# Persistent zero-padded buffers, smaller first LayerNorm batches and memsets on GpSimd in a linear-attention plus MLP kernel

## The chip, the cores and the metric

One core of a Trainium2 chip runs the whole kernel. The engines are TensorE (PE, with its weight loads shown apart as PEld), VectorE (DVE), ScalarE (ACT), GpSimd (POOL) and SyncE (SP), which issues the DMAs. The metric is the time of one execution in microseconds (us) on the device; of several executions the median is taken.

## The reference

The input x has 2048 rows of 640 bfloat16 values. Each row is normalised (mean and variance over 640, eps 1e-5), and the result xn goes into two branches that are added to x:

```
q, k, v  = xn @ wqkv                    # 32 heads of 20
pq, pk   = phi(q), phi(k)               # phi(t) = (t > 0 ? t + 1 : exp(t)) + 1e-6
kv, z    = sum over rows of pk v^T, of pk      # per head
A        = ((pq kv) / (pq z + 1e-6)) @ wo
B        = max(xn @ w1, 0) @ w2         # 640 -> 1728 -> 640
out      = x + A + B
```

## The kernel before, in words

Rows are worked on in 16 tiles of 128 rows; four tiles make a group of 512 rows. The 640 attention columns are cut into six groups of heads, five of 120 columns and one of 40, and the 1728 hidden columns of the MLP into 13 chunks of 128 and one of 64.

**Loads.** SP issues x tiles 0 to 3 one by one (L87), then wqkv (L89), then x in three pieces of four tiles (L91), then w1, w2 and wo. Rows of w2 and wo beyond the last real one are zeroed on POOL.

**Stage 1 and 2 (tiles).** `ln_stats(tg)` computes the statistics of four tiles on DVE: two `bn_stats` (L162) and one `bn_aggr` (L163) per tile, then for the four tiles together the inverse square root, as eps plus variance (`vpe`, L165), a shift and a multiply-add on the bits (`yi`, `y0i`), and three Newton steps of four operations each (L177 to L188). These are 15 short operations on 128x4 values, each needing the one before. `phase_a(t)` normalises a tile on DVE (`xn`, L198), transposes it with five PE matmuls against `ident` into PSUM (`tp`, L204) and copies it on ACT into `xnT` (L205). `phase_b(t)` computes k and v of the tile (ten matmuls each, L212 and L220), phi(k) with an exp on ACT (L227), a min on DVE (L229) and a max-add on DVE (`pk_all`, L230), and copies v into `v_aug` on ACT (L235, L241), which has one extra column of ones per head group so that the next stage also yields z. k_ps and v_ps share three PSUM buffers. So v_ps of tile t+1 takes the buffer of k_ps of tile t, free when `pk_all` of tile t is done, and k_ps of tile t+2 takes that of v_ps of tile t. In the text k_ps(4) is the k_ps of tile 4, and so on.

The loop goes over t with a lag of two tiles between phase a and phase b; `ln_stats` of group 1 stands in front of phase_a(1), of group 2 in front of phase_a(5), of group 3 in front of phase_a(9).

**Stage C.** For each head group, 16 matmuls accumulate kv over all tiles (L312). The result is masked into `KVmask` and `Zh`, which had been zeroed by DVE memsets (L270, L273). `hind`, `et` and `Amat` are 0/1 patterns made on POOL.

**Stage 3 (groups of 512 rows).** q and phi(q) (L341 to L358), the MLP's hidden chunks (`do_h`, L363 to L378), the denominator and its reciprocal (L384 to L398), the numerator (L403 to L416), and per tile the sum over 14 hidden chunks and six head groups into `o_ps` (L418 to L439), plus x, and the store. The operands of these matmuls are read at all 128 partitions, so wherever a tile has fewer real rows, `zero_pad` (L76) clears the rest. That happens on DVE each time for `pq` (L354), the last hidden chunk (L374), `rden` (L397) and `o` (L412).

**Order.** The planner (the tile framework) decides each engine's order when the kernel is built. Among the instructions whose inputs are ready in its own reckoning it takes the one that stands earliest in the program. So short work that stands late, such as the memsets of L270, is drawn forward into idle time, and steps of a dependent chain have other instructions between them.

Of the kernel before, what the change touches and what calls it, by code (L numbers as in the profile page):

```python
# [7 lines left out]
ALU = mybir.AluOpType  # L8
# [4 lines left out]
def kernel(  # L13
# [10 lines left out]
    nc = tc.nc  # L24
    bf16 = mybir.dt.bfloat16
# [4 lines left out]
    S, D = x2.shape  # L30
# [102 lines left out]

    xnT = xpool.tile([P, NC, S], bf16, name="xnT")

    kvin_ctx = ExitStack()
    kvin = kvin_ctx.enter_context(tc.tile_pool(name="kvin", bufs=1))
    ctxAB = ExitStack()
# [3 lines left out]
    pk_all = kvin.tile([P, NT, D], bf16, name="pk_all")  # L142
    v_aug = kvin.tile([P, NT, NG, GW + 1], bf16, name="v_aug")
    if D // GW > 0:
        nc.vector.memset(v_aug[:, :, 0 : D // GW, GW : GW + 1], 1.0)
    if NG > D // GW:
        gs, w = groups[-1]
        nc.vector.memset(v_aug[:, :, NG - 1, w : w + 1], 1.0)

    i32 = mybir.dt.int32  # L150
    lnp = ctxAB.enter_context(tc.tile_pool(name="lnp", bufs=2))
    mv_alls = {}
    rstds = {}

    def ln_stats(tg):
        mv_all = lnp.tile([P, TPG, nc.vector.BN_AGGR_DIM], f32, name="mv_all")
        for ti in range(TPG):
            t = tg * TPG + ti
            stats = wk1.tile([P, 2, nc.vector.BN_STATS_DIM], f32, name="stats")
            xr = x_all[:, t, :].rearrange("p (n f) -> p n f", n=2)  # L160
            for i in range(2):
                nc.vector.bn_stats(stats[:, i, :], xr[:, i, :])  # L162
            nc.vector.bn_aggr(mv_all[:, ti, :], stats[:])  # L163
        vpe = wk1.tile([P, TPG], f32, name="vpe")
        nc.vector.tensor_scalar(vpe[:], mv_all[:, :, 1], 1e-5, None, op0=ALU.add)  # L165
        yi = wk1.tile([P, TPG], i32, name="yi")
        nc.vector.tensor_single_scalar(
            yi[:], vpe[:].bitcast(i32), 1, op=ALU.arith_shift_right
        )
        y0i = wk1.tile([P, TPG], i32, name="y0i")  # L170
        nc.vector.tensor_scalar(
            y0i[:], yi[:], -1, 0x5F3759DF, op0=ALU.mult, op1=ALU.add
        )
        y = y0i[:].bitcast(f32)
        for it in range(3):
            t1 = wk1.tile([P, TPG], f32, name="nt1")
            nc.vector.tensor_tensor(t1[:], y, y, ALU.mult)  # L177
            t2 = wk1.tile([P, TPG], f32, name="nt2")
            nc.vector.tensor_tensor(t2[:], t1[:], vpe[:], ALU.mult)
            t3 = wk1.tile([P, TPG], f32, name="nt3")  # L180
            nc.vector.tensor_scalar(
                t3[:], t2[:], -0.5, 1.5, op0=ALU.mult, op1=ALU.add
            )
            if it < 2:
# [3 lines left out]
            nc.vector.tensor_tensor(yn[:], y, t3[:], ALU.mult)  # L188
            y = yn[:]
        mv_alls[tg] = mv_all  # L190
        rstds[tg] = yn

    def phase_a(t):
        tg, ti = divmod(t, TPG)
        mv_all = mv_alls[tg]
        rstd = rstds[tg]
        xn = wk1.tile([P, D], bf16, name="xn")
        nc.vector.tensor_scalar(  # L198
            xn[:], x_all[:, t, :], mv_all[:, ti, 0:1], rstd[:, ti : ti + 1],
            op0=ALU.subtract, op1=ALU.mult,  # L200
        )
        tp = ps_tp.tile([P, NC, P], bf16, name="tp")
        for c in range(NC):
            nc.tensor.transpose(tp[:, c, :], xn[:, c * P : (c + 1) * P], ident[:])  # L204
        nc.scalar.copy(xnT[:, :, t * P : (t + 1) * P], tp[:])  # L205
# [36 lines left out]

    LAG = 2
    ln_stats(0)
    for t in range(NT + LAG):
        if t < NT:
            if t % TPG == 1 and t // TPG + 1 < NTG:
                ln_stats(t // TPG + 1)
            phase_a(t)
        if t >= LAG:  # L250
            phase_b(t - LAG)
# [15 lines left out]
    for g, (gs, w) in enumerate(groups):  # L267
        h0 = gs // Dh
        kvm = const.tile([P, P], bf16, tag=f"kvm{g}", name=f"kvm{g}")
        nc.vector.memset(kvm[:], 0.0)  # L270
        KVmask.append(kvm)
        zh = const.tile([P, H], bf16, tag=f"zh{g}", name=f"zh{g}")
        nc.vector.memset(zh[:], 0.0)  # L273
        Zh.append(zh)
        hind = const.tile([P, H], bf16, tag=f"hind{g}", name=f"hind{g}")
        nc.gpsimd.memset(hind[:w, :], 1.0)
        nc.gpsimd.affine_select(  # L277
            out=hind[:w, :], in_=hind[:w, :], pattern=[[-Dh, H]],
            compare_op=ALU.is_ge, fill=0.0, base=Dh * h0, channel_multiplier=1,
        )  # L280
# [7 lines left out]
        nc.gpsimd.memset(et[:], 0.0)  # L288
# [36 lines left out]
    kvin_ctx.close()  # L325

    with ExitStack() as ctx3:
        qo = ctx3.enter_context(tc.tile_pool(name="qo", bufs=2))
        hp = ctx3.enter_context(tc.tile_pool(name="hp", bufs=2))
        wk2 = ctx3.enter_context(tc.tile_pool(name="wk2", bufs=3))  # L330
        opool = ctx3.enter_context(tc.tile_pool(name="opool", bufs=3))
# [3 lines left out]
        for tg in range(NTG):  # L335
            tsl = slice(tg * TG, (tg + 1) * TG)
            pq = []
            for g, (gs, w) in enumerate(groups):
                q_ps = psA.tile([P, 512], f32, tag="mm", name="q_ps")
                for c in range(NC):  # L340
                    nc.tensor.matmul(  # L341
                        q_ps[:w, :TG],
                        wqkv_sb[:, c, gs : gs + w],
                        xnT[:, c, tsl],
                        start=(c == 0), stop=(c == NC - 1),
                    )
                eq = wk2.tile([P, TG], bf16, name="eq")
                nc.scalar.activation(eq[:w, :], q_ps[:w, :TG], ACT.Exp)  # L348
                eq1 = wk2.tile([P, TG], bf16, name="eq1")
                nc.vector.tensor_scalar(  # L350
                    eq1[:w, :], eq[:w, :], 1.0, 1e-6, op0=ALU.min, op1=ALU.add
                )
                pqt = qo.tile([P, TG], bf16, tag=f"pq{g}", name=f"pq{g}")
                zero_pad(nc.vector, lambda lo, hi: pqt[lo:hi, :], w)  # L354
                nc.vector.scalar_tensor_tensor(
                    pqt[:w, :], in0=q_ps[:w, :TG], scalar=0.0, in1=eq1[:w, :],
                    op0=ALU.max, op1=ALU.add,
                )  # L358
                pq.append(pqt)
# [44 lines left out]
            for g, (gs, w) in enumerate(groups):  # L404
# [68 lines left out]
```

## Time and profile before

| what | value |
|---|---|
| median of 6 executions | 269.38 us (269.06 to 270.0) |
| the profiled execution | 269.81 us, span 268.1 us |
| PE busy | 248.6 us, 93% of the span |
| DVE busy | 133.2 us, 50% |
| ACT busy | 104.5 us, 39% |
| POOL busy | 13.1 us, 5% |
| first transpose on PE | 11.93 us |
| first k matmul | 13.91 us |
| end of the kv matmuls of stage C | about 71.5 us |

The profile is one execution, seen by the hardware profiler. The span runs from its first to its last instruction; the execution's time is a little longer than that. Times in timelines are counted from the span's start. In a row of forty digits each digit is the busy share of one fortieth of the span, 6.7 us, in tenths. A row of waits names the waiting engine and line, what released it, the total, the number of waits and the longest. The chain is followed back from the last instruction, at each step to what released it. In the table by stage each line is a stretch of time, its length, and the busy time and instruction count of PE, PEld, DVE, ACT and POOL, then the granted clock and the DMA share and rate.

### The profile page before, as it was taken

What the parts mean: (1) busy time and instruction counts of PE and PEld (TensorE: products, weight loads), DVE (VectorE), ACT (ScalarE), POOL (GpSimd) and SP (SyncE); (2) the same over time, 40 slices, a digit from 0 to 9 for tenths busy, and PEclk for the clock granted to TensorE, in tenths of its full rate; (3) what the DMA queues carried; (4) which work ended last, traced back from release to release, by engine and by line L of the source; (5) the groups of instructions that cost most, each with busy time, mean ns of one, the idle gap of its engine ahead of it and who ended that gap; (6) DMA issues with size and microseconds to landing.
All of it is one profiled execution on the core that took longest, in us unless ns stands there. A gap on an engine that the chain in (4) does not pass through costs nothing.

```text
span 268.1 us, 3982 instructions
## 1 busy us (share of the span) xinstructions
PE 248.6 (93%) x1609; PEld 132.6 (49%) x1609; DVE 133.2 (50%) x350; ACT 104.5 (39%) x179; POOL 13.1 (5%) x59
## 2 busy tenths in 40 slices
PE   0187899999999999999999999999999999999994
PEld 0154555656844445565444555544455564445552
DVE  6869996335795766128254511844341154235211
ACT  1153676665356660005666100465710035563000
POOL 8900000000000000000000000000000000000000
PEclk9999999999999999999999999999999999999999
DMA  6999900000000000000000000000001000000010
GB/s 202 390 388 375 187 5 2 0 4 0 4 0 0 2 0 24 27 24 24 0 2 0 26 27 24 24 2 0 0 0 51 24 24 4 0 0 0 27 49 24
DMA packets 8219, 13.19 MB, mean 49 GB/s; under 512 B 457, under 2 KB 6921, under 8 KB 8201
## 3 DMA queue, kind: packets, MB, share of 16 engines
q1 hardware_dynamic: 8201, 12.95, 14.5%
q8 instruction: 12, 0.20, 0.3%
q14 instruction: 6, 0.05, 0.1%
HBM read 10.32 MB, written 2.62 MB: 48 GB/s over the span
## 4 chain that ended last, share of the span: by engine, by line
PE 83%; DVE 10%; DMA 5%; SPq 1%; issue 0%; ACT 0%; DVEq 0%
PE h_ps L367 23%; PE o_ps L425 23%; PE q_ps L341 10%; PE o_ps L433 10%; DMA x_all<-in_A_x_dram 5%; PE v_ps L220 5%; PE k_ps L212 4%; DVE stats L162 3%; PE num_ps L410 2%; PE rep_ps L406 2%; DVE pk_all L230 2%; PE den_ps L386 2%; PE kv_ps L312 2%; DVE xn L198 1%; PE tp L204 1%; SPq L87 1%
## 5 line engine op out<-in xcount | busy, mean ns | idle before, releaser
L367 PE MATMUL h_ps<-xnT,w_sb 128*128 128x512 bf16 (+1 forms) x280 | 62.3, 380 | 0.0
L367 PEld LDWEIGHTS <-w_sb 128*128 128x128 bf16 (+1 forms) x280 | 26.7, 99 | 35.1 <-issue 5.1
L348 ACT ACTIVATE eq<-q_ps 120x512 bf16<-120x512 f32 (+1 forms) x24 | 14.3, 596 | 74.9 <-PE q_ps L341 74.9
L441 DVE TENSOR_TENSOR o_sb<-o_ps,x_all 128x640 bf16<-128x640 f32 x16 | 13.2, 825 | 53.4 <-PE o_ps L433 53.3
L341 PE MATMUL q_ps<-xnT,wqkv_sb 128*120 128x512 bf16 (+1 forms) x120 | 27.0, 379 | 0.3 <-ACT kvsb L318 0.3
L220 PE MATMUL v_ps<-wqkv_sb,xnT 128*128 128x512 bf16 (+1 forms) x160 | 24.5, 299 | 2.6 <-DVE pk_all L230 2.6
L395 DVE RECIPROCAL rdenf<-denp 32x512 f32<-32x512 f32 x4 | 13.4, 3341 | 25.6 <-ACT denp L391 25.6
L212 PE MATMUL k_ps<-wqkv_sb,xnT 128*128 128x512 bf16 (+1 forms) x160 | 25.3, 306 | 0.0
L341 PEld LDWEIGHTS <-wqkv_sb 128*120 128x120 bf16 (+1 forms) x120 | 14.7, 127 | 10.8 <-issue 1.8
L204 PE MATMUL tp<-ident,xn 128*128 128x128 bf16 x80 | 7.7, 236 | 12.9 <-POOL hind_977 L277 11.9
L220 PEld LDWEIGHTS <-xnT 128*128 128x128 bf16 x160 | 13.0, 98 | 12.1 <-issue 2.9
L212 PEld LDWEIGHTS <-xnT 128*128 128x128 bf16 x160 | 13.3, 100 | 10.1 <-issue 1.3
L162 DVE BATCH_NORM_STATS2 stats<-x_all 128x6 f32<-128x320 bf16 x32 | 14.1, 468 | 3.7 <-DMA x_all<-in_A_x_dram 3.7
L205 ACT COPY xnT<-tp 128x640 bf16<-128x640 bf16 x16 | 11.1, 707 | 11.7 <-PE tp L204 11.7
L235 ACT CAST v_aug<-v_ps 128x600 bf16<-128x600 f32 x16 | 10.5, 658 | 12.9 <-PE v_ps L220 12.9
L408 ACT CAST rep<-rep_ps 120x512 bf16<-120x512 f32 (+1 forms) x24 | 13.5, 580 | 2.3 <-PE rep_ps L406 1.6
L227 ACT ACTIVATE ek<-k_ps 128x640 bf16<-128x640 f32 x16 | 11.2, 703 | 7.1 <-PE k_ps L212 7.1
L204 PEld LDWEIGHTS <-xn 128*128 128x128 bf16 x80 | 5.6, 106 | 13.7 <-DVE xn L198 13.2
L198 DVE TENSOR_SCALAR xn<-x_all,mv_all,rstd 128x640 bf16<-128x640 bf16 x16 | 7.0, 454 | 0.3 <-PE tp L204 0.2
L312 PE MATMUL kv_ps<-v_aug,pk_all 128*120 128x121 bf16 (+1 forms) x96 | 5.1, 213 | 0.0
L312 PEld LDWEIGHTS <-pk_all 128*120 128x120 bf16 (+1 forms) x96 | 5.0, 128 | 0.1
L78 POOL MEMSET wo_sb<- 32x640 bf16 (+1 forms) x7 | 4.1, 626 | 0.2
(586 smaller groups left out, 444.9 us busy)
## 6 DMA issues: line engine op xcount, KB each, us to landing
out_dram<-o_sb SPq DMA_DIRECT2D x16, 160.0 KB, 1.8
wqkv_sb<-in_A_wqkv_dram SPq DMA_DIRECT2D x1, 2400.0 KB
w_sb<-in_B_w_dram SPq DMA_DIRECT2D x1, 2160.0 KB, 14.7
w_sb<-in_B_w_dram SPq DMA_DIRECT2D x1, 2080.0 KB, 22.3
x_all<-in_A_x_dram SPq DMA_DIRECT2D x3, 640.0 KB, 13.6
wo_sb<-in_A_wo_dram SPq DMA_DIRECT2D x1, 750.0 KB, 11.9
x_all<-in_A_x_dram SPq DMA_DIRECT2D x4, 160.0 KB, 2.6
w_sb<-in_B_w_dram SPq DMA_DIRECT2D x1, 80.0 KB, 18.4
```

What stands on the lines that cost most here:

```text
L162: nc.vector.bn_stats(stats[:, i, :], xr[:, i, :])
L204: nc.tensor.transpose(tp[:, c, :], xn[:, c * P : (c + 1) * P], ident[:])
L212: nc.tensor.matmul(k_ps[:, cs : cs + n], xnT[:, c, t * P : (t + 1) * P], wqkv_sb[:, c, D + cs : D + cs + n], start=(c == 0), stop=(c == NC ...
L220: nc.tensor.matmul(v_ps[:, cs : cs + n], xnT[:, c, t * P : (t + 1) * P], wqkv_sb[:, c, 2 * D + cs : 2 * D + cs + n], start=(c == 0), stop= ...
L312: nc.tensor.matmul(kv_ps[:w, 0 : w + 1], pk_all[:, t, gs : gs + w], v_aug[:, t, g, 0 : w + 1], start=(t == 0), stop=(t == NT - 1),)
L341: nc.tensor.matmul(q_ps[:w, :TG], wqkv_sb[:, c, gs : gs + w], xnT[:, c, tsl], start=(c == 0), stop=(c == NC - 1),)
L348: nc.scalar.activation(eq[:w, :], q_ps[:w, :TG], ACT.Exp)
L367: nc.tensor.matmul(h_ps[:m, :TG], w1_sb[:, c, fs : fs + m], xnT[:, c, tsl], start=(c == 0), stop=(c == NC - 1),)
L395: nc.vector.reciprocal(rdenf[:H, :], denp[:H, :])
L408: nc.scalar.copy(rep[:w, :], rep_ps[:w, :TG])
L425: nc.tensor.matmul(o_ps[:, cs : cs + n], hT[j][:, ti * P : (ti + 1) * P], w2_sb[:, j, cs : cs + n], start=(step == 0), stop=(step == nstep ...
L433: nc.tensor.matmul(o_ps[:, cs : cs + n], oT[g][:, ti * P : (ti + 1) * P], wo_sb[:, g, cs : cs + n], start=(step == 0), stop=(step == nstep ...
```

## The change

A new pool `pers` holds two sets of `pq`, `o`, `rden` and last hidden-chunk buffers for the whole kernel. Their padding rows are zeroed once, on POOL, right after `xnT` is allocated, and stage 3 takes set `tg % 2`. The 68 `zero_pad` calls' memsets of stage 3 fall away, and 34 on POOL take their place. The memsets of `v_aug`'s ones, of `kvm` and of `zh` go from DVE to POOL. The statistics are computed in five batches, of tiles 0-1, 2-3, 4-7, 8-11 and 12-15, with two Newton steps instead of three. A batch stands in front of the phase a of the tile before its first: batch 1 in front of phase_a(1), batch 2 in front of phase_a(3), batch 3 in front of phase_a(7), batch 4 in front of phase_a(11).

```diff
+    pers = ctx.enter_context(tc.tile_pool(name="pers", bufs=1))
+    pq_bufs, o_bufs, rden_bufs, hlast_bufs = [], [], [], []
+    for b in range(2):
+        pqb, ob = [], []
+        for g, (gs, w) in enumerate(groups):
+            tpq = pers.tile([P, TG], bf16, tag=f"pq{g}_{b}", name=f"pq{g}_{b}")
+            zero_pad(nc.gpsimd, lambda lo, hi, tpq=tpq: tpq[lo:hi, :], w)
+            pqb.append(tpq)
+            tob = pers.tile([P, TG], bf16, tag=f"ot{g}_{b}", name=f"ot{g}_{b}")
+            zero_pad(nc.gpsimd, lambda lo, hi, tob=tob: tob[lo:hi, :], w)
+            ob.append(tob)
...
+        trd = pers.tile([P, TG], bf16, tag=f"rden_{b}", name=f"rden_{b}")
+        zero_pad(nc.gpsimd, lambda lo, hi, trd=trd: trd[lo:hi, :], H)
...
+            zero_pad(nc.gpsimd, lambda lo, hi, thl=thl: thl[lo:hi, :], ml)
...
-        nc.vector.memset(v_aug[:, :, 0 : D // GW, GW : GW + 1], 1.0)
+        nc.gpsimd.memset(v_aug[:, :, 0 : D // GW, GW : GW + 1], 1.0)
...
-        nc.vector.memset(v_aug[:, :, NG - 1, w : w + 1], 1.0)
+        nc.gpsimd.memset(v_aug[:, :, NG - 1, w : w + 1], 1.0)
...
-    lnp = ctxAB.enter_context(tc.tile_pool(name="lnp", bufs=2))
+    lnp = ctxAB.enter_context(tc.tile_pool(name="lnp", bufs=3))
+    ln_batches = []
+    if NT >= 2:
+        ln_batches.append(list(range(0, 2)))
+        if NT >= TPG:
+            ln_batches.append(list(range(2, TPG)))
+            for tg in range(1, NTG):
+                ln_batches.append(list(range(tg * TPG, (tg + 1) * TPG)))
...
-    def ln_stats(tg):
+    def ln_stats(bi):
+        tiles = ln_batches[bi]
+        n = len(tiles)
...
-        for it in range(3):
+        NIT = 2
+        for it in range(NIT):
...
     ln_stats(0)
+    next_batch = 1
     for t in range(NT + LAG):
         if t < NT:
-            if t % TPG == 1 and t // TPG + 1 < NTG:
-                ln_stats(t // TPG + 1)
+            if next_batch < len(ln_batches) and t >= ln_batches[next_batch][0] - 1:
+                ln_stats(next_batch)
+                next_batch += 1
+            if tile_batch[t][0] >= next_batch:
+                ln_stats(next_batch)
+                next_batch += 1
             phase_a(t)
...
-        nc.vector.memset(kvm[:], 0.0)
+        nc.gpsimd.memset(kvm[:], 0.0)
...
-        nc.vector.memset(zh[:], 0.0)
+        nc.gpsimd.memset(zh[:], 0.0)
...
-        qo = ctx3.enter_context(tc.tile_pool(name="qo", bufs=2))
...
-                pqt = qo.tile([P, TG], bf16, tag=f"pq{g}", name=f"pq{g}")
-                zero_pad(nc.vector, lambda lo, hi: pqt[lo:hi, :], w)
+                pqt = pq_bufs[tg % 2][g]
...
-                ht = hp.tile([P, TG], bf16, tag=f"h{j}", name=f"h{j}")
-                zero_pad(nc.vector, lambda lo, hi: ht[lo:hi, :], m)
+                if m < P:
+                    ht = hlast_bufs[tg % 2]
+                else:
+                    ht = hp.tile([P, TG], bf16, tag=f"h{j}", name=f"h{j}")
...
-            rden = wk2.tile([P, TG], bf16, name="rden")
-            zero_pad(nc.vector, lambda lo, hi: rden[lo:hi, :], H)
+            rden = rden_bufs[tg % 2]
...
-                ot = qo.tile([P, TG], bf16, tag=f"o{g}", name=f"o{g}")
-                zero_pad(nc.vector, lambda lo, hi: ot[lo:hi, :], w)
+                ot = o_bufs[tg % 2][g]
```

More of the change, by code (lines that the diff above doesn't have):

```diff
@@ L134 @@
     xnT = xpool.tile([P, NC, S], bf16, name="xnT")
+    pers = ctx.enter_context(tc.tile_pool(name="pers", bufs=1))
[9 more added lines that the diff above has]
+            ob.append(tob)
+        pq_bufs.append(pqb)
+        o_bufs.append(ob)
+        trd = pers.tile([P, TG], bf16, tag=f"rden_{b}", name=f"rden_{b}")
+        zero_pad(nc.gpsimd, lambda lo, hi, trd=trd: trd[lo:hi, :], H)
+        rden_bufs.append(trd)
+        fsl, ml = ffc[-1]
+        if ml < P:
+            thl = pers.tile([P, TG], bf16, tag=f"hlast_{b}", name=f"hlast_{b}")
+            zero_pad(nc.gpsimd, lambda lo, hi, thl=thl: thl[lo:hi, :], ml)
+            hlast_bufs.append(thl)
     kvin_ctx = ExitStack()
@@ L144 @@
     if D // GW > 0:
-        nc.vector.memset(v_aug[:, :, 0 : D // GW, GW : GW + 1], 1.0)
+        nc.gpsimd.memset(v_aug[:, :, 0 : D // GW, GW : GW + 1], 1.0)
     if NG > D // GW:
         gs, w = groups[-1]
-        nc.vector.memset(v_aug[:, :, NG - 1, w : w + 1], 1.0)
+        nc.gpsimd.memset(v_aug[:, :, NG - 1, w : w + 1], 1.0)
     i32 = mybir.dt.int32
-    lnp = ctxAB.enter_context(tc.tile_pool(name="lnp", bufs=2))
+    lnp = ctxAB.enter_context(tc.tile_pool(name="lnp", bufs=3))
[7 more added lines that the diff above has]
+        else:
+            ln_batches.append(list(range(2, NT)))
+    else:
+        ln_batches.append(list(range(NT)))
+    tile_batch = {}
+    for bi, b in enumerate(ln_batches):
+        for pos, t in enumerate(b):
+            tile_batch[t] = (bi, pos)
     mv_alls = {}
     rstds = {}
-    def ln_stats(tg):
+    def ln_stats(bi):
+        tiles = ln_batches[bi]
+        n = len(tiles)
         mv_all = lnp.tile([P, TPG, nc.vector.BN_AGGR_DIM], f32, name="mv_all")
-        for ti in range(TPG):
-            t = tg * TPG + ti
+        for pos, t in enumerate(tiles):
             stats = wk1.tile([P, 2, nc.vector.BN_STATS_DIM], f32, name="stats")
@@ L162, in ln_stats @@
                 nc.vector.bn_stats(stats[:, i, :], xr[:, i, :])
-            nc.vector.bn_aggr(mv_all[:, ti, :], stats[:])
+            nc.vector.bn_aggr(mv_all[:, pos, :], stats[:])
         vpe = wk1.tile([P, TPG], f32, name="vpe")
-        nc.vector.tensor_scalar(vpe[:], mv_all[:, :, 1], 1e-5, None, op0=ALU.add)
+        nc.vector.tensor_scalar(vpe[:, :n], mv_all[:, :n, 1], 1e-5, None, op0=ALU.add)
         yi = wk1.tile([P, TPG], i32, name="yi")
         nc.vector.tensor_single_scalar(
-            yi[:], vpe[:].bitcast(i32), 1, op=ALU.arith_shift_right
+            yi[:, :n], vpe[:, :n].bitcast(i32), 1, op=ALU.arith_shift_right
         )
@@ L171, in ln_stats @@
         nc.vector.tensor_scalar(
-            y0i[:], yi[:], -1, 0x5F3759DF, op0=ALU.mult, op1=ALU.add
+            y0i[:, :n], yi[:, :n], -1, 0x5F3759DF, op0=ALU.mult, op1=ALU.add
         )
-        y = y0i[:].bitcast(f32)
-        for it in range(3):
+        y = y0i[:, :n].bitcast(f32)
+        NIT = 2
+        for it in range(NIT):
             t1 = wk1.tile([P, TPG], f32, name="nt1")
-            nc.vector.tensor_tensor(t1[:], y, y, ALU.mult)
+            nc.vector.tensor_tensor(t1[:, :n], y, y, ALU.mult)
             t2 = wk1.tile([P, TPG], f32, name="nt2")
-            nc.vector.tensor_tensor(t2[:], t1[:], vpe[:], ALU.mult)
+            nc.vector.tensor_tensor(t2[:, :n], t1[:, :n], vpe[:, :n], ALU.mult)
             t3 = wk1.tile([P, TPG], f32, name="nt3")
             nc.vector.tensor_scalar(
-                t3[:], t2[:], -0.5, 1.5, op0=ALU.mult, op1=ALU.add
+                t3[:, :n], t2[:, :n], -0.5, 1.5, op0=ALU.mult, op1=ALU.add
             )
-            if it < 2:
+            if it < NIT - 1:
                 yn = wk1.tile([P, TPG], f32, name="nyn")
@@ L187, in ln_stats @@
                 yn = lnp.tile([P, TPG], f32, name="rstd")
[L188 to L191, printed above, removed]
+            nc.vector.tensor_tensor(yn[:, :n], y, t3[:, :n], ALU.mult)
+            y = yn[:, :n]
+        mv_alls[bi] = mv_all
+        rstds[bi] = yn
     def phase_a(t):
-        tg, ti = divmod(t, TPG)
-        mv_all = mv_alls[tg]
-        rstd = rstds[tg]
+        bi, ti = tile_batch[t]
+        mv_all = mv_alls[bi]
+        rstd = rstds[bi]
         xn = wk1.tile([P, D], bf16, name="xn")
@@ L372, in do_h @@
                     )
-                ht = hp.tile([P, TG], bf16, tag=f"h{j}", name=f"h{j}")
-                zero_pad(nc.vector, lambda lo, hi: ht[lo:hi, :], m)
+                if m < P:
+                    ht = hlast_bufs[tg % 2]
+                else:
+                    ht = hp.tile([P, TG], bf16, tag=f"h{j}", name=f"h{j}")
                 nc.scalar.activation(
```

## The prediction, made before the changed kernel was run

> **What bounds the kernel now.** I read the page first, then the waits of TensorE, then the chain that ended last, then the start in order of time, and last a table of busy time by stage.
>
> ```profile
> PE 248.6 (93%) x1609; PEld 132.6 (49%) x1609; DVE 133.2 (50%) x350; ACT 104.5 (39%) x179; POOL 13.1 (5%) x59
> ...
> PE   0187899999999999999999999999999999999994
> PEld 0154555656844445565444555544455564445552
> DVE  6869996335795766128254511844341154235211
> ```
>
> The page's row of digits for PE puts the idle time of TensorE (PE) in the first six slices, about 40 us, and DVE is full in just those slices. The waits say for whom PE waits:
>
> ```profile
> PE tp L204 <- POOL hind_977 L277: 11.9, 1, 11.9
> PE v_ps L220 <- DVE pk_all L230: 2.6, 3, 1.9
> PE tp L204 <- DVE xn L198: 0.8, 1, 0.8
> PE q_ps L341 <- ACT kvsb L318: 0.3, 1, 0.3
> ```
>
> The POOL name in the first line is a coincidence of times: its real condition is the first xn, which DVE finished at 11.74. The table by stage shows that after 43 us PE never waits again except those 0.3 us:
>
> ```profile
> 24.00:28.00 4.00, 3.44 (x25) 1.64 (x22) 4.00 (x18) 2.12 (x4) 0.00 (x0) 1.00 1.07 357
> 28.00:32.00 4.00, 3.51 (x35) 2.31 (x36) 4.00 (x20) 2.71 (x7) 0.00 (x0) 1.00 1.04 177
> ...
> 76.00:120.00 44.00, 44.00 (x261) 21.80 (x259) 23.44 (x55) 15.34 (x24) 0.00 (x0) 1.00 0.03 12
> 120.00:170.00 50.00, 50.00 (x289) 25.50 (x287) 21.84 (x44) 17.73 (x28) 0.00 (x0) 1.00 0.04 15
> ```
>
> So the last 225 us are TensorE work that this change does not touch, and whatever PE gains or loses by about 43 us moves the end by the same amount. The chain tells what sets the first 43 us:
>
> ```profile
> 3.13 12.49 DMA x_all<-in_A_x_dram
> 15.65 1.28 DVE stats L162 x3
> ...
> 20.38 0.82 DVE pk_all L230
> ...
> 26.71 0.82 DVE pk_all L230
> 27.69 0.39 DVE stats L162
> 28.08 0.35 DVE xn L198
> ...
> 41.30 1.52 PE v_ps L220 x10
> ```
>
> The second group of x (tiles 4 to 7) lands at 15.65, and from there to 41.30 the chain is DVE's own queue: DVE is the bound there, not PE.
>
> **The change, part by part.**
>
> *Stage 3 (after 71.7 us).* Per group of 512 rows 7 pads of pq, 7 of o, 2 of rden and 1 of the last h leave DVE: 17 x 4 = 68 memsets at 0.27 us (the rows of 32x256 and 64x256 uint32), 18.4 us of DVE time. PE is at 44.00 of 44.00 and 50.00 of 50.00 there, so the gain is nothing. Two persistent buffers stand where the pools had two (rden had three, and is read by PE within a few us of being written), so no new wait on a buffer is of a length that PE would see. Cost 0.
>
> *Memsets from DVE to POOL.* Two of v_aug, six kvm and six zh ran on DVE from 1.25 to 2.00, while DVE waited for x until 3.08: gain 0 there. On POOL: 34 pads of 32 or 64 rows x 512, placed behind ident (L122, L123) and ahead of v_aug, Amat, hind, et, kvm and zh. Seven wo_sb memsets of 640 columns take 4.26 us together, 0.61 each; 128 columns take 0.15 from start to start; between them 512 columns come to 0.49. 34 x 0.49 = 16.8 us. POOL ends at 14.03 now; so about 14.0 + 16.8 + 1.4 (kvm, zh, v_aug at 0.05 to 0.15) = 32 us. Their first readers are kv_ps at 66.35 (v_aug) and the mask at 67.84, so 34 us of cover remain. ident, which the first transpose needs, is ahead of the pads and ready near 6.5 to 7.0, still before the first xn. DMAs do not move: SP issues the same list.
>
> *Start.* Statistics of two tiles instead of four before the first chain: bn_aggr of tile 1 ends at 5.37, that of tile 3 at 6.83, so 1.46 earlier. The chain from vpe (6.87) to xn (11.30) is 15 operations in 4.43 us, 0.295 each; one Newton step less is 4 operations, 1.18 us. The remaining bn_stats of tiles 2 and 3 and the second batch's chain now stand between the steps; about 0.8 us back. First xn near 9.5 instead of 11.30. But k_ps needs wqkv: x tiles 0 to 3 and wqkv are 3.11 MB, and the DMA rates from 2 us on add up to that at about 11.1 us; in the profile k_ps started at 13.91 without a recorded wait. So it lands between 11.1 and 13.9, and k_ps of tile 0 starts between 11.7 (first xn plus the present 2.2 us from xn to k_ps) and 13.9. I take 12.9. A clock that is still slow there (k_ps of tile 0 took 2.46 us against 1.52 for the next) can shift later by a us; it has cover, as the next wait shows.
>
> *DVE from 15.65.* This is what counts. Statistics of tiles 4 to 7 are now emitted at t=3 instead of t=1, behind pk_all of tile 0. So pk_all(0) no longer queues behind all eight bn_stats, and the 1.89 us wait of v_ps(1) goes. What is late next is v_ps(2), which needs the PSUM buffer of k_ps(1) and so pk_all(1): statistics 4.2 us and pk_all(0) with its min 1.06 end at 20.9; pk_all(1) 1.06 more, 22.0 to 22.3 instead of 24.4. Then xn(4): now the chain of 15 took 19.88 to 27.61, 7.73 us, with three pk_all and seven bn_stats between its steps. Without pk_all(0) it is 6.6 us, 0.44 a step; 11 steps are 4.8, from 20.9 to 25.7. With the order of fillers unknown I take 26.0, 2.0 us before the present 28.00.
>
> *Contention.* POOL was silent after 14.03; now it writes through this stretch, to 32 us. What that costs DVE is seen at the start:
>
> ```profile
> 6.88 0.19 POOL L288 MEMSET et_929<- 128x128 bf16 x1
> 7.03 0.28 POOL L259 TENSOR_SCALAR_AFFINE_SELECT Amat<-Amat 6x120 bf16<-6x120 bf16 x1
> 7.14 0.50 DVE L167 TENSOR_SCALAR yi<-vpe 128x4 int32<-128x4 int32 x1
> ...
> 37.58 0.17 DVE L181 TENSOR_SCALAR nt_573<-nt_571 128x4 f32<-128x4 f32 x1
> ```
>
> The same 0.16 us operations take up to 0.50 beside a busy POOL. Alone, ten chain steps from 37.58 take 0.20 each; at the start 0.295, so 0.1 a step. Ends for the stretch to xn(4): nothing (the wo_sb memsets ran beside bn_stats of 0.48, no longer than later ones), or one full memset, 0.49, for each of 5 chain tensor_scalars, 3 mins of ek and one xn: 4.4 us. I take 0.1 x 11 = 1.1, nearest to the row. xn(4) then starts at 27.1.
>
> The Trainium skill, in "SBUF — State Buffer", section "Who interferes with whom", speaks against the move: GpSimd and VectorE share a port pair, an exclusive lock held for a whole instruction, against VectorE operations in a two-port mode. The rows agree in kind (yi 0.50 against 0.16). By the page a held operation would wait half a memset on average, estimated 9 x 0.25 = 2.2 us, and the time would be 268.7. It also says that a tensor_tensor is held only by a GpSimd instruction that reads, which memsets do not; that part would lower it.
>
> *Sum.* PE ends v_ps(3) near 26.4 and then waits for xn(4): 27.1 + 0.44 (xn) + 0.05 + 0.3 (transposes) + 0.1 + 0.71 (copy) = 28.7 for k_ps(4), against 30.41 now: 1.7, less 0.28 for one transposed tile that is still to come: 1.4. Of the 0.38 wait at 41.30 (behind pk_all, with all DVE work by then about 1 us shorter) I take all away: 1.8 us. The profiled execution took 269.81 (span 268.1 and 1.7 around it), 0.43 over the median of 269.38; it would become 268.0, and the median, with the same 1.8 off, 267.6.
>
> **Rivals.**
>
> *A. The port decides (slower).* If POOL's pads cost DVE 4.4 us instead of 1.1, everything from xn(4) on is 3.3 us later than in the sum: a loss of 1.5 where the sum has a gain of 1.8, so 270.9. It turns where the added DVE time between 15.65 and xn(4) passes 1.1 + 1.8 = 2.9 us. For it: yi and nt_148 at 0.50 and 0.47. Against it: the four xn beside POOL took 1.76, hardly more than alone.
>
> *B. v_aug's ones come too late (same).* They now stand behind the pads, done near 23.7. If the copies into v_aug (L235) were ordered behind them, k_ps(2), which needs the buffer of v_ps(0), would wait from about 19.5 to 24.4; k_ps(2), v_ps(2), k_ps(3), v_ps(3) at 1.36 each end at 29.9, 3.5 later than in the sum, of which the wait for xn(4) covers 2.0. That leaves a gain of 0.3: 269.1. Against it: ones and copies touch different columns, and xnT's copy of tile 2 (14.15) ran while k_ps(0) read interleaved columns of the same tile, so strided neighbours are told apart.
>
> *C. Nothing (same).* If the planner puts statistics of tiles 4 to 7 ahead of pk_all(0) as before and contention takes the shorter chain back, only the first transposes come earlier, and x at 15.65 hides them: 269.2 to 269.5.
>
> *D. More (faster).* No contention and no new wait: all of 1.89, 0.29, 0.75 and 0.38 go, 3.3 us, and up to 0.9 from an earlier wqkv (the slow clock takes the rest of that): 265.2.
>
> **How the numbers follow.** The forecast (266.0 to 268.8) 0.58, D 0.11, C 0.10, B 0.05, A 0.16, in which I count whatever else DVE's new order may cost. Under 0.2%, 0.54 us, this kernel's measurement can't be told from no change. Faster: forecast and D, 0.69; same, C and B, 0.15; slower, A, 0.16. The range runs from D's 265.2 to A's 270.9, the two bounds of the unknown costs; what lies outside is some of A's and D's own spread.
>
> **What the changed profile would show.** DVE's memsets gone after 67 us and PE's windows there as full as before; POOL busy to about 32 us; first xn near 9.5; k_ps of tile 0 between 11.7 and 13.9; no wait of v_ps(1) on pk_all; v_ps(2) near 22.3; xn(4) near 27.1, with chain tensor_scalars above 0.16 us; k_ps(4) near 28.7. The prediction is wrong if POOL's pads stretch DVE by 3 us, if a copy of ACT waits for POOL, or if DVE's new order makes a later tile's xn late (tiles 8 to 11 are now planned two tiles later, and k_ps(8) must not wait).

## The result: slower by 0.56%

The changed kernel takes 270.63 us (median of 8 executions, 269.66 to 272.09), the kernel before beside it 269.21 us (16 executions, 267.63 to 270.1). The ratio is 1.0056 with a 95% interval of 1.0032 to 1.0081: about 1.5 us slower, where 1.8 us faster was forecast. 267.6 us is missed by 3 us; the range, 265.2 to 270.9, still holds the time.

The profiled execution of the changed kernel took 270.24 us (span 268.5), only 0.43 more than the one of before (269.81). That is an accident of the two profiles: the second group of x landed at 14.76 in this one and at 15.65 in the other, and the loads are the same. From that landing to the first `q_ps` matmul of stage 3, the kernel before took 71.75 - 15.65 = 56.10 us and the changed one 72.08 - 14.76 = 57.32: 1.22 us more.

The page of the changed kernel, with the engines' sums and the rows of forty digits:

```profile
PE 250.0 (93%) x1609; PEld 132.9 (49%) x1609; DVE 115.9 (43%) x263; ACT 104.5 (39%) x179; POOL 33.8 (13%) x107
...
PE   0395999999999999999999999999999999999994
...
DVE  4989995334480551117153211724341154235211
...
POOL 8999920000000000000000000000000000000000
```

DVE lost 17.3 us of work (133.2 to 115.9), POOL gained 20.7 and is now busy through the fifth slice (33.6 us) and a little beyond, beside a DVE that is as full there as it was. The table by stage (per engine its busy time and instruction count, in the order PE, PEld, DVE, ACT, POOL) shows what DVE's relief in stage 3 is worth:

```profile
76.00:120.00 44.00, 44.00 (x258) 21.71 (x257) 13.99 (x20) 15.46 (x25) 0.00 (x0) 1.00 0.04 12
120.00:170.00 50.00, 50.00 (x293) 25.59 (x291) 17.52 (x25) 17.51 (x28) 0.00 (x0) 1.00 0.04 14
```

PE is at 44.00 of 44.00 and 50.00 of 50.00, as before; DVE's figure fell from 23.44 to 13.99 and from 21.84 to 17.52, for nothing. All that matters is still in the first 43 us. There PE waits for:

```profile
PE tp L243 <- DVE xn L237: 12.1, 4, 10.8
PE v_ps L259 <- DVE pk_all L269: 2.0, 1, 2.0
PE k_ps L251 <- DVE pk_all L269: 0.3, 1, 0.3
PE q_ps L384 <- ACT kvsb L362: 0.3, 1, 0.3
```

The waits on `pk_all` were three of 2.6 us together and are now two of 2.3: the 1.89 us wait of v_ps(1) has gone, but one of 1.98 us of v_ps(2) has come. PE's timeline shows how:

```profile
19.41 1.52 PE L259 MATMUL v_ps<-wqkv_sb,xnT 128*128 128x512 bf16 x10
21.28 1.52 PE L251 MATMUL k_ps<-wqkv_sb,xnT 128*128 128x512 bf16 x10 [0.35 <-DVE pk_all L269]
24.78 1.24 PE L259 MATMUL v_ps<-wqkv_sb,xnT 128*128 128x512 bf16 x5 [1.98 <-DVE pk_all L269]
26.68 0.45 PE L243 MATMUL tp<-ident,xn 128*128 128x128 bf16 x5 [0.66 <-DVE xn L237]
...
27.59 0.45 PE L243 MATMUL tp<-ident,xn 128*128 128x128 bf16 x5 [0.18 <-DVE xn L237]
27.88 1.52 PE L251 MATMUL k_ps<-wqkv_sb,xnT 128*128 128x512 bf16 x10
...
30.88 1.52 PE L251 MATMUL k_ps<-wqkv_sb,xnT 128*128 128x512 bf16 x10
```

v_ps(1) ran from 19.41 to 20.93, while pk_all(0) was still reading k_ps(0) (20.41 to 21.23). So it no longer takes the buffer of k_ps(0), as it did in the kernel before; k_ps(2) takes it now, and waits for pk_all(0). The planner gives out the three buffers anew in each kernel. The transposes at 26.68 and 27.59 are those of tiles 4 and 5, and the k_ps at 27.88 and 30.88 are k_ps(3) and k_ps(4). From the landing to k_ps(4) it is 16.12 us (30.88 - 14.76); it was 14.76 us before (30.41 - 15.65).

The chain that ended last is almost all DVE's queue as before, from the landing of x to a `pk_all`:

```profile
3.12 11.61 DMA x_all<-in_A_x_dram
14.76 1.28 DVE stats L200 x3
...
20.41 0.82 DVE pk_all L269
...
23.91 0.82 DVE pk_all L269
...
26.27 0.37 DVE xn L237
...
34.60 0.82 DVE pk_all L269
35.47 1.52 PE v_ps L259 x10
```

pk_all(0) starts 5.65 us after the landing. It was 4.73 us before (20.38 - 15.65), and by the prediction it was to come earlier, no longer behind all eight `bn_stats`. Between landing and pk_all(0) DVE still runs all eight `bn_stats` of tiles 4 to 7, and three more where the kernel before had two. The one more is some 0.4 of the 0.92 us; two timelines show what the rest is, DVE's first:

```profile
19.45 0.41 DVE L268 TENSOR_SCALAR ek_299<-ek 128x640 bf16<-128x640 bf16 x1
19.78 0.57 DVE L205 TENSOR_SCALAR yi<-vpe 128x4 int32<-128x4 int32 x1
20.41 0.82 DVE L269 SCALAR_TENSOR_TENSOR pk_all<-k_ps,ek_299 128x640 bf16<-128x640 f32 x1
...
22.62 0.47 DVE L220 TENSOR_SCALAR nt_331<-nt_329 128x4 f32<-128x4 f32 x1
...
23.20 0.60 DVE L268 TENSOR_SCALAR ek_376<-ek 128x640 bf16<-128x640 bf16 x1
```

and POOL's at the same time:

```profile
18.67 0.52 POOL L78 MEMSET pq_1_148<- 32x512 bf16 x1
19.14 0.54 POOL L78 MEMSET ot_1_150<- 32x512 bf16 x1
```

With POOL silent, in the kernel before, `yi` took 0.16 and `ek` 0.32 in this stretch. Beside the pads they take up to 0.57 and 0.60. `pk_all`, one of whose two inputs is in PSUM, keeps its 0.82, and the `bn_stats` their mean of 0.468.

### The profile page after: what moved, and what is told of

It reads as the page before. It is cut to its first block, busy times and chain, and to the rows that moved or that the text cites. A ratio compares the mean times of both kernels' runs of the same rounds, so it can differ in the third digit from the quotient of the medians.

```text
span 268.5 us, 3943 instructions
## 1 busy us (share of the span) xinstructions
PE 250.0 (93%) x1609; PEld 132.9 (49%) x1609; DVE 115.9 (43%) x263; ACT 104.5 (39%) x179; POOL 33.8 (13%) x107
## 4 chain that ended last, share of the span: by engine, by line
PE 86%; DVE 8%; DMA 4%; SPq 1%; issue 0%; ACT 0%
PE h_ps L409 23%; PE o_ps L467 23%; PE q_ps L384 10%; PE o_ps L475 10%; PE v_ps L259 6%; PE k_ps L251 5%; DMA x_all<-in_A_x_dram 4%; DVE stats L200 3%; PE num_ps L453 2%; PE rep_ps L449 2%; PE den_ps L430 2%; PE kv_ps L356 2%; DVE pk_all L269 1%; PE tp L243 1%; SPq L87 1%; DVE mv_all L201 0%
## 5 line engine op out<-in xcount | busy, mean ns | idle before, releaser
L259 PE MATMUL v_ps<-wqkv_sb,xnT 128*128 128x512 bf16 (+1 forms) x160 | 25.1, 303 | 2.1 <-DVE pk_all L269 2.0
L259 PEld LDWEIGHTS <-xnT 128*128 128x128 bf16 x160 | 13.3, 99 | 12.1 <-issue 3.1
L243 PE MATMUL tp<-ident,xn 128*128 128x128 bf16 x80 | 7.8, 236 | 12.1 <-DVE xn L237 12.1
L237 DVE TENSOR_SCALAR xn<-x_all,mv_all,rstd 128x640 bf16<-128x640 bf16 x16 | 7.6, 487 | 0.1
L455 DVE TENSOR_TENSOR ot_0_107<-num_ps,rep 120x512 bf16<-120x512 f32 x2 | 1.4, 692 | 8.9 <-ACT rep L451 4.5
L455 DVE TENSOR_TENSOR ot_1_138<-num_ps,rep 120x512 bf16<-120x512 f32 x2 | 1.4, 692 | 8.9 <-PE num_ps L453 8.9
## 6 DMA issues: line engine op xcount, KB each, us to landing
x_all<-in_A_x_dram SPq DMA_DIRECT2D x3, 640.0 KB, 12.9
```

Source lines behind the costliest of these rows:

```text
L259: nc.tensor.matmul(v_ps[:, cs : cs + n], xnT[:, c, t * P : (t + 1) * P], wqkv_sb[:, c, 2 * D + cs : 2 * D + cs + n], start=(c == 0), stop= ...
```

## The experiments

The theory after the result: the pads on POOL stretch DVE's short operations while DVE is the bound, and the gain that should have paid for it isn't there. The rival: the new batches of statistics put DVE in a worse order, and the pads are harmless. Each ratio is against the kernel before on the same chip.

**The pads alone.** The kernel before with persistent buffers and POOL pads; statistics and the other memsets untouched.

```diff
+            zero_pad(nc.gpsimd, lambda lo, hi, tpq=tpq: tpq[lo:hi, :], w)
...
-                zero_pad(nc.vector, lambda lo, hi: pqt[lo:hi, :], w)
+                pqt = pq_bufs[tg % 2][g]
```

> The kernel before with the persistent buffers and their 34 pads on POOL alone; statistics in four batches with three Newton steps, and the memsets of v_aug, kvm and zh on DVE, as before. P (POOL's pads hold DVE in the stretch from the landing of x tiles 4-7 to about 34 us): slower by 0.8 to 2 us, 270.2 to 271.4, with mins of ek and chain tensor_scalars at 0.4 to 0.6 us there. O (the new statistics batches order DVE's work worse, POOL is harmless): no change, 269.2 to 269.6. K (the slow clock at the first k and v matmuls makes the loss): no change, 269.2 to 269.6, since the start is as before.

271.6 against 269.02: 1.008 (1.0049 to 1.0111). The pads alone lose as much as the whole change, or more. In the profile they took 57.57 us from the landing to `q_ps`, against 56.10. The planned order moved a little too: eleven `bn_stats` ahead of pk_all(0) instead of ten.

**The statistics alone.** The five batches and two Newton steps, no other part.

```diff
-        for it in range(3):
+        NIT = 2
+        for it in range(NIT):
```

> The kernel before with the five statistics batches and two Newton steps alone; pads and memsets on DVE as before. P: faster by 0.8 to 1.8 us, 267.6 to 268.6, pk_all(1) about 1 us earlier after the landing than in the changed kernel. O: slower by about 1.4, 270.4 to 271.2. K: between, 269.4 to 270.4, with the first k and v matmuls as slow as in the changed kernel (about 5 us together against 4.0).

269.13 against 269.02: 0.9996 (0.9977 to 1.0016). The part that was to gain 2.9 us before contention gains nothing that can be told. So the rival falls, and a second question opens: where did that gain go? The PE timeline has one answer at the start:

```profile
10.59 1.25 PE L221 MATMUL tp<-ident,xn 128*128 128x128 bf16 x10 [10.59 <-POOL hind L299]
12.19 0.71 PE L221 MATMUL tp<-ident,xn 128*128 128x128 bf16 x5 [0.35 <-DVE xn L215]
14.19 2.83 PE L229 MATMUL k_ps<-wqkv_sb,xnT 128*128 128x512 bf16 x10 [1.28 <-DMA wqkv_sb<-in_A_wqkv_dram]
16.81 2.86 PE L237 MATMUL v_ps<-wqkv_sb,xnT 128*128 128x512 bf16 x10
```

The first transposes come 1.3 us earlier than before and buy a wait: wqkv lands only at 14.19. And the first twenty matmuls then take 2.83 and 2.86 where the kernel before needed 2.46 and 1.52.

Further on it has a second answer. DVE did get faster: xn(4) came 10.50 us after the landing (26.45 - 15.95), where the kernel before needed 12.35 (28.00 - 15.65). But k_ps(4) came 14.65 us after it (30.60 - 15.95), against 14.76:

```profile
26.94 0.45 PE L221 MATMUL tp<-ident,xn 128*128 128x128 bf16 x5 [1.22 <-DVE xn L215]
...
27.82 1.31 PE L229 MATMUL k_ps<-wqkv_sb,xnT 128*128 128x512 bf16 x9
28.96 1.52 PE L237 MATMUL v_ps<-wqkv_sb,xnT 128*128 128x512 bf16 x9
...
30.60 1.52 PE L229 MATMUL k_ps<-wqkv_sb,xnT 128*128 128x512 bf16 x10
```

In PE's planned order the transposes of tile 4 now stand ahead of k_ps(3) and v_ps(3). PE waits 1.22 us for xn(4) and then has all these matmuls still to do. The kernel before did k_ps(3) first, at 25.78, and waited behind it. From xn(4) to k_ps(4) it is 4.15 us instead of 2.41, so of the 1.85 us that DVE gained at xn(4) 0.11 were left at k_ps(4).

**The whole change, with the pads written late.** The pads go to POOL after stage 1 and 2, as a multiply of the last columns of xnT by 0, which makes each wait for them.

```diff
-            zero_pad(nc.gpsimd, lambda lo, hi, tpq=tpq: tpq[lo:hi, :], w)
+            late_pads.append((tpq, w))
...
+            nc.gpsimd.tensor_scalar(
+                tl[lo:hi, :], xnT[lo:hi, 0, S - TG : S], 0.0, None, op0=ALU.mult
+            )
```

> The changed kernel with its 34 pads written by POOL as 0 times the last 512 columns of xnT, so that none can start before the last tile is normalised, about 58 us; everything else as changed, so hind, et, kvm and zh still run on POOL at the start and end near 16 us. P: as e2, 267.6 to 268.8. O: as the changed kernel, 270.4 to 271.2. K: as the changed kernel within 0.3 us, or at most 0.5 better. If the late pads were not done before the denominator at 86 us, PE would show a wait there.

269.18 against 269.02: 1.001 (0.9987 to 1.0033). With the same buffers and the same statistics, the loss of 0.56% is down to 0.1%, not told from none. The pads ran from 59 to 112 us at 1.49 us each, three times as dear, and cost nothing that shows there. DVE does the same 41 operations between the landing and xn(4) as in the changed kernel, in 10.51 us (26.66 - 16.15) instead of 11.43 (26.19 - 14.76). But the planned orders differ here too (ten `bn_stats` ahead of pk_all(0), eleven in the changed kernel), so this run alone does not part the pads from the plan.

**Two Newton steps alone.** The kernel before with `range(2)`.

> The kernel before with two Newton steps instead of three, nothing else. P: DVE's chain from the landing to xn(4) is four steps shorter, 1 to 2 us earlier, 268.0 to 268.8. O: the same gain. K: the first xn is 1.2 us earlier and the clock eats some of it: 268.4 to 269.4.

268.94 against 269.02: 0.9996 (0.9977 to 1.0014). xn(4) came at 25.75, which is 2.25 us before the 28.00 of the kernel before, and k_ps(4) at 30.19 against 30.41. v_ps(2) starts at 24.48, where it did (24.43). Behind it PE has three blocks of ten matmuls at 1.36 and three tiles of transposes at 0.28 to do before k_ps(4), 4.92 us. So v_ps(2) alone puts k_ps(4) at 29.40 or later here and at 29.35 or later before, and an earlier xn(4) can win little more than PE's wait for it, 0.75. It won less, because PE waited for it again, 0.51 us: here too the transposes of tile 4 stand ahead of k_ps(3). What v_ps(2) waits for is pk_all(1). It started at 23.61 here and at 23.55 before.

**Extra transposes against the slow start.** Two Newton steps, and 36 and 18 transposes of ident in front of those of tiles 0 and 2, to have PE busy before k_ps(0).

```diff
+        for r in range({0: 36, 2: 18}.get(t, 0)):
+            nc.tensor.transpose(tp[:, 0, :], ident[:], ident[:])
```

> e4 (two Newton steps, else as before) with PE kept busy until wqkv lands: 36 more transposes of ident ahead of the first tile's five and 18 ahead of the third tile's, into the same PSUM tiles, overwritten by the real ones. K (the slow clock of the first k and v matmuls ate what the shorter chain gained): the first k and v take about 3.2 us together instead of 5.7, and the time falls by 0.8 to 1.8 us against e4, 267.2 to 268.2. Q (PE's second and third v_ps wait for pk_all, whose place in DVE's planned order has not moved, so the slow clock has cover): v_ps(1) waits about 1.9 us for pk_all(0) as before, and the time is e4's, 268.6 to 269.3.

273.98 against 268.88: 1.0188 (1.0152 to 1.0224), near none of the expectations. k_ps(0) and v_ps(0) did run in 1.52 each. But the planned order of DVE had moved as well: 19 `bn_stats` now stood between the landing and pk_all(0), ten in the kernel before, and it started at 23.52. The PE timeline:

```profile
24.40 2.82 PE L222 MATMUL v_ps<-wqkv_sb,xnT 128*128 128x512 bf16 x10 [6.81 <-DVE pk_all L232]
```

In the table by stage the granted clock (the first figure after the five engines) fell during that wait:

```profile
18.00:22.00 4.00, 0.00 (x0) 0.00 (x0) 4.00 (x21) 0.33 (x1) 0.00 (x0) 0.76 1.02 383
22.00:26.00 4.00, 1.60 (x4) 0.55 (x4) 4.00 (x21) 0.00 (x0) 0.00 (x0) 0.50 1.06 368
```

It says nothing clean about the slow start, but points at the place of pk_all(0) in DVE's order.

**That place held by hand.** Two Newton steps, and the statistics of tiles 6 and 7 held behind pk_all(0), those of tiles 8 to 11 behind pk_all(2), those of 12 to 15 behind pk_all(6). No pads on POOL.

```diff
+            if t == 1:
+                ln_bn(1, range(0, 2))
+            if t == 3:
+                with tc.issue_after(pk_ins[0].ins):
+                    ln_bn(1, range(2, 4))
+                ln_chain(1)
+            if t == 5:
+                with tc.issue_after(pk_ins[2].ins):
+                    ln_bn(2, range(TPG))
+                    ln_chain(2)
```

> e4 with DVE's order changed and nothing else: statistics of tiles 6 and 7 are queued behind pk_all(0), those of tiles 8 to 11 behind pk_all(2), those of tiles 12 to 15 behind pk_all(6). Q: pk_all(0) starts near 18.0 and pk_all(1) near 22 instead of 20.4 and 23.6, v_ps(2) near 22.7 instead of 24.5, and the time is 267.2 to 268.3. K, or the landing of x as the only bound: 268.6 to 269.3.

267.14 against 268.88: 0.9942 (0.9917 to 0.9968). So there is a gain, 1.6 us, once DVE's order is held. pk_all(0) started 3.03 us after the landing (16.78 - 13.75), behind four `bn_stats` instead of ten, and neither v_ps(1) nor v_ps(2) (21.11) waited for `pk_all`. With the statistics of tiles 8 to 11 out of its way as well, xn(4) came 8.80 us after the landing (22.55 - 13.75), and k_ps(4) 13.37 (27.12 - 13.75) instead of 14.76. PE's last wait ahead of k_ps(4) was for xn(4), 0.92 us at 23.06. What each of the three holds is worth by itself was not measured.

**wqkv's k and v columns first.** Two Newton steps; the q columns of wqkv load after x.

```diff
+    nc.sync.dma_start(wqkv_sb[:, :, D : 3 * D], wqkv_view[:, :, D : 3 * D])
...
+    nc.sync.dma_start(wqkv_sb[:, :, 0:D], wqkv_view[:, :, 0:D])
```

> e4 with wqkv loaded in two pieces: the k and v columns (1.64 MB) where wqkv was, the q columns (0.82 MB) behind the last piece of x. Theory D (the first 43 us hang on the landings: the first k matmul on wqkv, DVE on x tiles 4-7): wqkv's first piece lands near 12, x tiles 4-7 near 13.6, each about 2.1 us (0.82 MB at 0.39 MB per us) earlier, and the end comes 1.5 to 2.3 us earlier, 266.8 to 267.6. If the landings are covered: 268.6 to 269.3.

268.61 against 268.88: 0.9987 (0.9966 to 1.0009). Nothing by itself: k_ps(0) no longer waits for wqkv (13.27, no wait), and the second group of x landed at 12.30, but pk_all(0) still stands behind the statistics, fifteen `bn_stats` later, at 19.50.

**Both.** That load order and the order held.

> e6 and e7 together. Q and D both right: the gains nearly add, since DVE's queue starts at the landing: 265.5 to 266.8. Only one of them right: as that one alone, 266.8 to 268.3.

266.22 against 268.88: 0.991 (0.9881 to 0.994). The number is better than the held order's alone (0.9942), but the intervals overlap.

**The pads on POOL under a held order.** This is the test of the pads that the moving plan cannot blur: the held order plus persistent buffers and the 34 POOL pads. DVE's and PE's instructions of stages 1 and 2 stand in the same order as without the pads.

> e6 (two Newton steps, DVE's order held) with the persistent buffers and their 34 pads on POOL at the start. DVE's and PE's orders through stage 2 are those of e6, instruction by instruction, so only what runs beside them differs. P (POOL's memsets hold DVE): slower than e6 by 1 to 2.5 us, 268.2 to 269.8, with mins, chain tensor_scalars and xn longer by 0.1 to 0.5 us each until POOL ends near 32 us. If e1 was slow because the planner's order had moved: as e6, 266.8 to 267.5.

268.76 against 269.52: 0.9985 (0.9965 to 1.0005), against 0.9942 without the pads, which ran on another chip: 0.43%, 1.2 us lost, with intervals that just touch. The next experiment, on one chip with this one, parts them. The same DVE operations, first without pads:

```profile
16.33 0.33 DVE L235 TENSOR_SCALAR ek<-ek 128x640 bf16<-128x640 bf16 x1 [0.59 <-ACT ek L233]
...
19.53 0.17 DVE L172 TENSOR_SCALAR vpe<-mv_all 128x4 f32<-128x4 f32 x1
19.74 0.17 DVE L174 TENSOR_SCALAR yi<-vpe 128x4 int32<-128x4 int32 x1
...
20.05 0.16 DVE L178 TENSOR_SCALAR y0i<-yi 128x4 int32<-128x4 int32 x1
20.24 0.82 DVE L236 SCALAR_TENSOR_TENSOR pk_all<-k_ps,ek 128x640 bf16<-128x640 f32 x1
20.98 0.15 DVE L184 TENSOR_TENSOR nt<-y0i 128x4 f32<-128x4 f32 x1
```

then with them:

```profile
17.45 0.71 DVE L257 TENSOR_SCALAR ek<-ek 128x640 bf16<-128x640 bf16 x1
...
21.03 0.61 DVE L194 TENSOR_SCALAR vpe<-mv_all 128x4 f32<-128x4 f32 x1
21.68 0.52 DVE L196 TENSOR_SCALAR yi<-vpe 128x4 int32<-128x4 int32 x1
...
22.29 0.57 DVE L200 TENSOR_SCALAR y0i<-yi 128x4 int32<-128x4 int32 x1
22.47 0.82 DVE L258 SCALAR_TENSOR_TENSOR pk_all<-k_ps,ek 128x640 bf16<-128x640 f32 x1
23.21 0.15 DVE L206 TENSOR_TENSOR nt<-y0i 128x4 f32<-128x4 f32 x1
```

Only the `tensor_scalar`s are stretched, by 0.35 to 0.44 us each; `pk_all` and `tensor_tensor` are not. From landing to xn(4) it is 9.63 us (25.17 - 15.54) against 8.80 (22.55 - 13.75), though the 8.80 hold a 0.59 us wait for ACT that the 9.63 do not.

**The same, with the pads late.** The held order, the persistent buffers, the pads as in the third experiment.

> e9 with the pads written late, as in e3 (0 times the last columns of xnT, after 58 us). P: as e6, 266.8 to 267.5. If the persistent buffers themselves cost something: as e9.

267.85 against 269.52: 0.9929 (0.9904 to 0.9953), as good as without pads and buffers (0.9942), and its interval is clear of that of the early pads, 0.9965 to 1.0005. By the medians early pads cost 0.9 us, by the ratios 0.56%, 1.5 us. xn(4) came 8.08 us after the landing (22.94 - 14.86), with no wait for ACT in between: 1.55 us sooner than the 9.63 of the early pads, for the same operations in the same order. The persistent buffers cost nothing that shows; when the pads are written does.

**Extra transposes under the held order.** The held order without pads, and the transposes of the fifth experiment.

> e6 with the extra transposes of e5 (36 ahead of tile 0's, 18 ahead of tile 2's); DVE's order is e6's, and PE's apart from them, which in e5 they were not. K (the slow clock of the first k and v costs time): the first k and v matmuls take 2.9 us together instead of 3.7 to 5.0, and the time falls by 0.5 to 1.5 us, 265.6 to 266.7. If DVE's statistics and chain to xn(4) still cover it: as e6, 266.8 to 267.5.

266.48 against 269.52: 0.9901 (0.9868 to 0.9935). k_ps(0) and v_ps(0) took 1.52 each instead of the 2.30 and 1.52 of the held order. Against its 0.9942 the intervals overlap, so a gain from the transposes is not shown.

**All three.** The held order, k and v columns first, extra transposes; two Newton steps, no pads on POOL.

> e8 (two Newton steps, DVE's order held, k and v columns of wqkv loaded first) with the extra transposes of e11. K: 0.5 to 1.5 us under e8, 264.7 to 265.8. Otherwise as e8, 266.0 to 266.5.

265.56 (265.17 to 265.93) against 269.52: 0.9859 (0.9831 to 0.9887). This version beats both kernels, by 3.8 us the one before. Of PE's waits behind its first instruction, 1.2 us in two waits are left for xn, 0.2 us for `pk_all` and 0.3 twice for ACT.

## Why the prediction was wrong

**The bound: right.** The first 43 us, DVE's queue from the landing of x, set the end; stage 3 is full PE in both kernels.

**Stage 3: right.** 68 memsets left DVE, and no time.

**Memsets to POOL, their cover: right.** The first transpose did not wait for ident, POOL ended at 35.46 (32 forecast), and no reader was late.

**Start: wrong in worth.** The first xn came at 10.25 (9.5 forecast; 9.91 with the statistics alone, 8.98 with the pads late). k_ps(0) was taken at 12.9 out of 11.7 to 13.9; the lower bound should have been 12.1, since 9.5 is the start of xn and the 2.2 us were counted from its end (13.91 - 11.74). It came at 13.12, but in five of the experiments' profiles it waited for wqkv and not for xn, to 13.08, 13.92, 14.19, 14.26 and 14.38: mostly at the upper bound or past it. An earlier xn cannot win there. "It has cover" held for the slow start, because v_ps(2) waited 1.98 us for pk_all(1) behind it: k_ps(0) and v_ps(0) together took 2.87 + 2.15 here, against 2.46 + 1.52. That took back the 0.79 by which k_ps(0) was earlier: the next transposes stand at 17.78, before at 17.57.

**DVE from 15.65: this step failed.** The prediction said that statistics emitted at t=3 stand "behind pk_all of tile 0. So pk_all(0) no longer queues behind all eight bn_stats". They stand later in the program, but the planner takes the earliest one among the instructions that are ready in its reckoning, and its order has the statistics first; that it reckoned pk_all(0)'s inputs later is what this suggests. DVE ran eleven `bn_stats` between the landing and pk_all(0). Behind it the sum has only the 1.06 us of pk_all(1) with its min. From the one to the other it was 3.50 us (20.41 to 23.91), with four more `bn_stats` in between. So pk_all(1) ended at 24.73, not at 22.0 to 22.3, though x had landed 0.89 us earlier than in the profile from which the forecast was made, and v_ps(2) came at 24.78, not 22.3. With the 4.92 us of PE work behind it, this alone puts k_ps(4) at 29.70 or later; 28.7 was forecast. Rival C named just this condition; it had 0.10. The sign "no wait of v_ps(1) on pk_all" came true by luck: v_ps(1) got another buffer, and pk_all(0) was not earlier. The held order, which puts pk_all(0) ahead of half of the eight and also holds back the statistics of tiles 8 to 11, gains 1.6 us; the batches as written, or two Newton steps, measured 0.9996, between 0.6 us gained and 0.4 lost.

**xn(4): right in time, and the step from it to k_ps(4) failed too.** It came at 26.19, 11.43 us after the landing (forecast 27.1, 11.45 after it; before 12.35). (Eight `bn_stats` stood between the steps of the old chain, not seven; the sum does not use the count.) The sum went from xn(4) to k_ps(4) in 1.6 us, because "PE ends v_ps(3) near 26.4 and then waits for xn(4)". With v_ps(2) at 24.78 that is false. Besides, PE's planned order has the transposes of tiles 4 and 5 ahead of k_ps(3). PE waited 0.66 and 0.18 us for xn(4) and xn(5), and then still had k_ps(3), v_ps(3) and the transposes of tile 6 to do. So k_ps(4) came at 30.88, 4.69 us after xn(4). Counted from the landing that is 16.12 us: 13.05 was forecast (28.7 - 15.65), and 14.76 was the time before. The statistics alone show the same order on PE, and the same loss of what xn(4) gained. So does the held order: xn(4) came 8.80 us after the landing there, 2.65 sooner than was forecast, and k_ps(4) 13.37, still 0.32 later than was forecast. The last term, the wait of 0.38 us at 41.30, did go.

**Contention: right in kind and about in size.** 1.1 us was taken at xn(4), from bounds of 0 and 4.4. The same 41 operations up to xn(4) took 0.9 us more in the changed kernel than in the two versions without early pads (11.43 against 10.50 and 10.51), and the held order puts it at 1.55 (9.63 against 8.08). At the end of the kernel, the late pads give back 0.46% (1.0056 to 1.001), 1.2 us, with intervals that just touch, and the held order puts it at 0.9 to 1.5. Rival A had the mechanism of the loss, with a price of 4.4 and 2.9 us as the point where it decides. That point stood on a gain of 2.9 that was not there; with a gain of nothing, 1.2 us were enough. The pads alone cost 0.8% (1.3 to 3.0 us); how much of the surplus is the longer chain of three Newton steps under the pads and how much a shifted plan is open.

The Trainium skill, "SBUF — State Buffer", section "Who interferes with whom", says that `tensor_scalar` can enter a two-port mode in which it and GpSimd hold each other up, that a DVE operation with at most one input in SBUF and outside these modes is not held, and that a `tensor_tensor` with both inputs in SBUF is held only by a GpSimd instruction that reads. The rows agree: the `tensor_scalar`s are stretched, while `pk_all`, which has one input in PSUM, and the `bn_stats` are not. `tensor_tensor` stayed at 0.14 to 0.16 beside the pads from the landing on. When POOL had come to its `affine_select`s, which read, one took 0.37, though others there kept 0.14 and 0.15 (DVE timeline of the changed kernel):

```profile
32.60 0.37 DVE L216 TENSOR_TENSOR nt_526<-nyn 128x4 f32<-128x4 f32 x1
```

The estimate from the page, half a memset for each of nine operations, was 2.2 us at xn(4); 0.9 to 1.55 were measured there, nearer to the row's 1.1.

**Rival B** is refuted: ACT copied into v_aug at 17.98, and POOL wrote its ones at 24.79.

## What to carry to other kernels

An engine that idles is no free place for memsets if it shares something with the engine that bounds that stretch: put them where the bounding engine is not DVE, and move nothing for the sake of a DVE that is not the bound (18.4 us here, worth 0). Before counting on a shorter chain or an earlier start, ask what lands or stands last there: here a weight load, matmuls that PE's order had put behind the transposes, and a `pk_all` that the planner kept behind statistics until they were held back by hand. Where a planner orders the work, a place later in the program is not a place later on the engine: an edit's worth is decided by the order that comes out.

## What was not expected of the hardware

- The second group of x landed between 13.75 and 16.15 us in profiles with one and the same list of loads. That moves the end of single profiled executions by more than most effects here; from the landing on they can be compared.
- k_ps(0) and v_ps(0) together took between 3.8 us (the held order) and 5.7 (two Newton steps) without extra transposes, while the granted clock read 1.00 in the changed kernel's profile, where they took 5.0. With 54 transposes ahead of them they took 1.52 + 1.52 in all three kernels that had these.
- The granted clock can fall behind short waits. In the profile with pads under the held order, PE waited 1.32 us up to 23.35 and 1.30 up to 25.67, and the clock went to 0.50 (table by stage):

```profile
24.00:26.00 2.00, 0.70 (x6) 0.33 (x5) 1.82 (x7) 0.00 (x0) 1.95 (x9) 0.88 1.06 364
26.00:28.00 2.00, 2.00 (x16) 1.55 (x15) 2.00 (x6) 1.31 (x3) 2.00 (x12) 0.50 1.11 341
28.00:30.00 2.00, 2.00 (x12) 0.97 (x11) 2.00 (x8) 0.87 (x4) 2.00 (x14) 0.77 1.04 200
```

k_ps(3) took 2.15 us there instead of 1.52. Four of that kernel's twelve executions have a mean clock of 0.991 to 0.993 and took 269.05 to 270.62; the other eight took 268.58 to 268.84, still some 0.8 us over the late pads' median of 267.85. In the changed kernel's profile PE waited 1.98 and 0.66 us in the same stretch, and the clock stayed at 1.00. Four of its timed executions, at 0.991 or 0.992, took 270.42 to 272.09; the other four took 269.66 to 270.79, with a median of 270.3, 1.1 us over the kernel before. So a part of the 1.5 us goes with the lower clock.
